# Chunk attention and a cosine router on one core: q moved from the GpSimd queue to the SP queue, the first loads reordered, the table fill moved

## The chip, the cores and the metric

The kernel runs on one core of one Trainium2 chip. The metric is the device time of one execution in microseconds. A core has five engines that run side by side, each with its own instruction stream: TensorE (PE) for matrix products, VectorE (DVE), ScalarE (ACT), GpSimd (POOL), and SyncE (SP), which here does nothing but issue transfers. All transfers run on 16 DMA engines that the queues share. A transfer issued by SP runs on the hardware queue, `q1` in the profile; one issued by GpSimd runs on the software queue, `q0`.

## What is computed

Two blocks follow each other. Attention within chunks of 64 rows, for 8 batches of 8 heads, 576 rows and 64 columns:

```python
batch, n_heads, seq, head_dim = (8, 8, 576, 64)
...
scores = scale * np.matmul(q_c, k_c.transpose(0, 1, 2, 4, 3))   # chunks of 64 rows
scores = scores - np.max(scores, axis=-1, keepdims=True)
attn = np.exp(scores)
attn = attn / (np.sum(attn, axis=-1, keepdims=True) + 1e-09)
out = np.matmul(attn, v_c)
```

The result, as 4608 tokens of 512 columns, goes to a router that sends each token to one of eight experts:

```python
logits = xn @ en.T / tau                   # normalized tokens and expert vectors
expert_idx = np.argmax(logits, axis=1)
...
for e in range(E):                         # E = 8, w1: 512 x 1024, w2: 1024 x 512
    mask = expert_idx == e
    h = np.maximum(x[mask] @ w1[e], 0.0)
    out[mask] = gate_w[mask, None] * (h @ w2[e])
```

Everything is float32.

## The kernel before

The attention stage walks over 36 tiles of 128 tokens, two chunks each. A batch of 576 rows is four and a half tiles. The tile of k and that of q hold all eight heads of 128 rows, with four buffers each, so that up to four tiles can be on their way. k is issued by SP, q by GpSimd. v is held for a whole batch, in two buffers that take turns, and loaded with one transfer for each head:

```python
tc.tile_pool(name="qk", bufs=4) as qk_p
...
def load_qk(t):
    for src, nm, eng in ((k, "kx", nc.sync), (q, "qx", nc.gpsimd)):
        x = qk_p.tile([P, H, Dh], FP32, tag=nm, name=nm)
        ...
            eng.dma_start(
                out=x[done : done + n],
                in_=src[b, :, s : s + n, :].rearrange("h p d -> p h d"),
            )
...
def load_v(b):
    t = v_sb[b % 2]
    for h in range(H):
        r0 = CH * (h % 2)
        nc.sync.dma_start(
            out=t[r0 : r0 + CH, h // 2, :, 0:Dh],
            in_=v[b, h].rearrange("(c k) d -> k c d", k=CH),
        )
    v_t[b] = t
```

In DRAM a row of q, k or v of one head is 64 floats, 256 bytes, so each of these transfers is made of pieces of 256 bytes. A tile of k or q is 1024 such pieces, 256 KB; v of one head of one batch is 576 pieces, 144 KB.

One pass of the main loop works on several tiles at different depths. It turns k and q of tile t+3 on TensorE (line 199), which frees their buffers, and loads tile t+7; it takes the scores of tile t+2 and the values of tile t, whose result x it writes to DRAM from GpSimd's queue. After the last tile, weights of the experts are loaded on the SP queue:

```python
for t in range(-3, NT + 3):
    if 0 <= t < NT:
        turn_a(t)
    if t + 3 < NT:
        turn_qk(t + 3)
        if t + 7 < NT:
            load_qk(t + 7)
        elif t + 7 == NT:
            load_first(w1_sb, w1_rows, KD, 0, nc.sync)
            load_first(w2_sb, w2_rows, KF, 0, nc.sync)
    ...
    if 0 <= t + 2 < NT:
        scores(t + 2)
    ...
    if 0 <= t < NT:
        values(t)                  # ends with the store of x, on GpSimd's queue
        b = (2 * t + 2) // NCB + 1
        if b not in v_t and b < B:
            load_v(b)              # the next batch, when this one begins
    ...
    put(1 if t < NT - 2 else 2)    # writes routed tokens into the table, from GpSimd
    if t == -2:
        turn_experts()
    if t == 0:
        clear_spots()
```

`clear_spots` fills the table `spots` in DRAM (2.3 MB) with a number that stands for "no row", by one transfer on the SP queue. The router's entries, of 64 bytes each, are then written over it by `put`; the first come six passes after t = 0. The start ahead of the loop:

```python
nc.sync.dma_start(out=emb, in_=moe_expert_emb)
nc.sync.dma_start(out=tau_sb, in_=moe_tau.unsqueeze(0).to_broadcast([E, 1]))
for t in range(2):
    load_qk(t)
norm_experts()
for x in v_sb:
    nc.vector.memset(x[:, :, :, Dh : Dh + 1], 1.0)
load_v(0)
for t in range(2, 4):
    load_qk(t)
load_v(1)
constants()
```

When all tokens are routed, the table is read by gathers on GpSimd's queue, which also loads the second set of weights, and the expert stage works through blocks of 128 tokens: `hidden` (line 635), `turn_h` (line 656) and `result` (line 668) on TensorE.

Of the kernel before, what the change touches and what calls it, by code (L numbers as in the profile page):

```python
# [19 lines left out]
CH = 64  # L20
# [5 lines left out]
def kernel(  # L26
# [11 lines left out]
    nc = tc.nc  # L38
    B, H, S, Dh = q.shape
# [7 lines left out]
    NCB = S // CH  # L47
# [32 lines left out]
    def load_first(buf, rows, n, i, eng):  # L80

        for s in range(2):
            e = (0, E - 1)[s]
            eng.dma_start(out=buf[s][i], in_=rows[:, e * n : e * n + n, :])
# [8 lines left out]
    with (  # L93
# [38 lines left out]
        def constants():  # L132
            nc.gpsimd.iota(tok_i, pattern=[[P, NT]], base=0, channel_multiplier=1)
            nc.gpsimd.iota(io_i, pattern=[[1, NST]], base=0, channel_multiplier=0)
            nc.gpsimd.iota(part_i, pattern=[[0, 1]], base=0, channel_multiplier=1)
            make_upper_triangular(nc, sltb, val=1.0, diag=False)
            nc.gpsimd.memset(onesb, 1.0)
            nc.gpsimd.memset(empty.bitcast(I32), NO_ROW)
            nc.gpsimd.memset(ones, 1.0)
            nc.gpsimd.memset(before, 0.0)  # L140
            nc.gpsimd.memset(jump[:, 1], 1.0)
            nc.gpsimd.memset(nb[:, 0:1], float((SPARE + N) // G))
            nc.gpsimd.tensor_copy(io, io_i)
            nc.gpsimd.tensor_copy(at, part_i)
            nc.gpsimd.tensor_scalar(pref, io[:, 0:E], -1.0, float(E), ALU.mult, ALU.add)
            nc.gpsimd.tensor_scalar(e_base, io[:, 0:E], float(N), None, ALU.mult)
            nc.gpsimd.tensor_scalar(second, at, float(G), None, ALU.is_ge)

            nc.gpsimd.tensor_scalar(at, at, 1.0 / G, None, ALU.mult)
            nc.gpsimd.tensor_tensor(at, at, second, ALU.subtract)  # L150
            nc.gpsimd.tensor_scalar(step, second, -2.0, 1.0, ALU.mult, ALU.add)
            nc.gpsimd.tensor_scalar(e_0, second, float(E - 1), None, ALU.mult)
            for x in xin_sb:
                nc.vector.memset(x, 0.0)
# [11 lines left out]
        qk_t, qkT, v_t, st = {}, {}, {}, {}  # L166

        def load_qk(t):

            for src, nm, eng in ((k, "kx", nc.sync), (q, "qx", nc.gpsimd)):  # L170
                x = qk_p.tile([P, H, Dh], FP32, tag=nm, name=nm)
                done = 0
                while done < P:
                    b, s = divmod(t * P + done, S)
                    n = min(P - done, S - s)
                    eng.dma_start(  # L176
                        out=x[done : done + n],
                        in_=src[b, :, s : s + n, :].rearrange("h p d -> p h d"),
                    )
                    done += n  # L180
                qk_t[nm, t] = x.rearrange("p h d -> p (h d)")

        def load_v(b):

            t = v_sb[b % 2]
            for h in range(H):
                r0 = CH * (h % 2)
                nc.sync.dma_start(  # L188
                    out=t[r0 : r0 + CH, h // 2, :, 0:Dh],
                    in_=v[b, h].rearrange("(c k) d -> k c d", k=CH),  # L190
                )
            v_t[b] = t

        def turn_qk(t):
            for nm in ("kx", "qx"):
                a = qk_t.pop((nm, t))
                ps = ps_t.tile([P, NPAIR, P], FP32, tag="tr", name="tr")
                for i in range(NPAIR):
                    nc.tensor.transpose(ps[:, i], a[:, i * P : i * P + P], ident)  # L199
                x = wk.tile([P, NPAIR, P], FP32, tag=nm + "T", name=nm + "T")  # L200
                if nm == "kx":
                    nc.scalar.copy(x, ps)
                else:
                    nc.vector.tensor_copy(x, ps)
                qkT[nm, t] = x
# [27 lines left out]
        def weights(t):  # L233
            a = st[t]["a"]
            nc.scalar.activation(a, a, AF.Exp, scale=scale)

        def turn_a(t):
            d = st[t]
            ps = ps_t.tile([P, NPAIR, P], FP32, tag="tr", name="tr")
            for i in range(NPAIR):  # L240
                nc.tensor.transpose(ps[:, i], d["a"][:, i].rearrange("p r k -> p (r k)"), ident)  # L241
            aT = wk.tile([P, NPAIR, P], FP32, tag="aT", name="aT")
            nc.scalar.copy(aT, ps)
            d["aT"] = aT
# [31 lines left out]
        def turn_x(t):  # L276
            d = st[t]
            ps = ps_t.tile([P, KD, P], FP32, tag="tr", name="tr")
            for c in range(KD):
                nc.tensor.transpose(ps[:, c], d["x"][:, c * P : c * P + P], ident)  # L280
            xT = wk.tile([P, KD, P], FP32, tag="xT", name="xT")
            nc.scalar.copy(xT, ps)  # L282
            d["xT"] = xT

        def logits(t):
            d = st.pop(t)
            for c in range(KD):
                nc.tensor.matmul(  # L288
                    rt_ps[:, 0, batch_of[t][1]],
                    lhsT=d["xT"][:, c],  # L290
                    rhs=enT[:, c],
                    start=(c == 0),
                    stop=(c == KD - 1),
                )
# [74 lines left out]
        def put(n):  # L369

            for at, m in to_put[:n]:
                ins = nc.gpsimd.indirect_dma_start(  # L372
                    out=spots,
                    out_offset=bass.IndirectOffsetOnAxis(ap=at, axis=0),
                    in_=m,
                    in_offset=None,
                    bounds_check=SPARE - 1,
                    oob_is_err=False,
                )
                tc.declare_no_dep(ins.ins, group="spots", reason="each token has its own place")  # L380
                tc.add_to_no_dep_group("spots", ins.ins)
            del to_put[:n]
# [73 lines left out]
        def norm_experts():  # L456

            junk = one.tile([P, D], FP32, tag="junk", name="junk")
            nc.scalar.activation(junk[0:E], emb, AF.Square, accum_out=emb_sq)
            nc.scalar.activation(emb_n, emb_sq, AF.Sqrt)  # L460
            nc.vector.tensor_scalar(emb_n, emb_n, 1e-6, None, ALU.add)
            nc.vector.reciprocal(emb_n, emb_n)
            nc.vector.reciprocal(tau_sb, tau_sb)
            nc.vector.tensor_scalar(emb, emb, emb_n, tau_sb, ALU.mult, ALU.mult)

        def turn_experts():
# [2 lines left out]
                nc.tensor.transpose(ps[:, c, 0:E], emb[:, c * P : c * P + P], ident[0:E, 0:E])  # L469
            nc.vector.tensor_copy(enT, ps[:, :, 0:E])  # L470

        nc.sync.dma_start(out=emb, in_=moe_expert_emb)
        nc.sync.dma_start(out=tau_sb, in_=moe_tau.unsqueeze(0).to_broadcast([E, 1]))
        for t in range(2):
            load_qk(t)
        norm_experts()
        for x in v_sb:
            nc.vector.memset(x[:, :, :, Dh : Dh + 1], 1.0)
        load_v(0)
        for t in range(2, 4):  # L480
            load_qk(t)
        load_v(1)
        constants()
        ends = {sum(sizes[: b + 1]) - 1: b for b in range(len(sizes))}
        for t in range(-3, NT + 3):
# [10 lines that stand above are left out]
            if t == NT:  # L496
                turn_x(t - 1)
            if 0 <= t - 2 < NT:
                logits(t - 2)
            if 0 <= t + 2 < NT:  # L500
                scores(t + 2)
            if t - 3 in ends:
                place(ends[t - 3])
            if 0 <= t - 1 < NT - 1:
                turn_x(t - 1)
            if 0 <= t < NT:
                values(t)
                b = (2 * t + 2) // NCB + 1
                if b not in v_t and b < B:
                    load_v(b)  # L510
            if 0 <= t + 2 < NT:
                weights(t + 2)
            if t - 2 in ends:
                pick(ends[t - 2])

            put(1 if t < NT - 2 else 2)
            if t == -2:
                turn_experts()
            if t == 0:
                clear_spots()  # L520
        groups()
        places(0, XBUF + 1)
# [241 lines left out]
```

## Time and profile before

| | |
|---|---|
| median of three runs | 806.37 us |
| lowest and highest | 802.37 and 807.18 us |
| span of the profiled run | 810.2 us |
| TensorE busy | 743.9 us, 92% of the span |
| hardware queue q1 | 101,136 packets, 84.18 MB |
| software queue q0 | 16,528 packets, 47.17 MB |
| HBM read and written | 383.07 MB and 21.80 MB |

The page gives the busy time of each engine and then cuts the span into 40 equal slices; a digit is the busy share of a slice in tenths. `PEclk` is the clock that TensorE was granted, `DMA` the mean busy share of the 16 DMA engines, `GB/s` what they moved. Packets of two queues on one DMA engine can be open at the same time, so shares of two queues can add up to over 100%. The timeline lists an engine's instructions in order, with the idle time before each and what ended it.

### The profile page before, as it was taken

The numbers are of one execution on the slowest core, as the hardware profiler recorded it, in microseconds if no ns is written. First come the engines' busy times: TensorE is split into PE (matmuls) and PEld (weight loads), VectorE is DVE, ScalarE is ACT, GpSimd is POOL, SyncE is SP. The second block draws the span as 40 slices with busy tenths as digits, with TensorE's granted clock in tenths as the row PEclk, the third lists the DMA queues.
The fourth block names the chain that finished last, engine by engine and source line by source line (L and its number), as shares of the span: only waits on it lengthen the run. The fifth ranks groups of instructions, "written<-read, shape, count | busy, mean of one in ns | idle before, by whom it ended". The sixth has DMA issues, their size and how long they took to land.

```text
span 810.2 us, 15342 instructions
## 1 busy us (share of the span) xinstructions
PE 743.9 (92%) x6033; PEld 367.7 (45%) x6033; DVE 251.7 (31%) x703; ACT 290.7 (36%) x520; POOL 221.3 (27%) x270
## 2 busy tenths in 40 slices
PE   2799999985569999999999999999999999999994
PEld 2688888874124333343343333343333343333331
DVE  2467777775221121121121121121121122122100
ACT  3345455441142243243243243333334334334102
POOL 4235556545420211211211311311211221221220
PEclk9999999995778999999999999999999999999998
DMA  9999999993670100115583416688530444312140
GB/s 177 234 264 246 238 251 234 258 399 133 233 247 1 51 27 27 53 59 202 189 305 131 155 61 229 253 328 323 169 118 27 144 144 131 140 44 79 72 150 9
DMA packets 117739, 132.37 MB, mean 163 GB/s; under 512 B 79860, under 2 KB 83252, under 8 KB 117664
## 3 DMA queue, kind: packets, MB, share of 16 engines
q1 hardware_dynamic: 101136, 84.18, 35.9%
q0 software_dynamic: 16528, 47.17, 18.4%
q8 instruction: 49, 0.80, 0.4%
q14 instruction: 26, 0.21, 0.1%
HBM read 383.07 MB, written 21.80 MB: 500 GB/s over the span
## 4 chain that ended last, share of the span: by engine, by line
PE 83%; DMA 4%; issue 3%; DVE 3%; SPq 3%; POOL 1%; ACT 0%; POOLq 0%; DVEq 0%; ACTq 0%
PE y_ps L668 31%; PE h_ps L635 29%; PE ht_ps L656 4%; PE rt_ps L288 4%; PE pv L255 3%; PE tr L280 3%; PE tr L199 3%; PE sc L215 2%; SPq L188 2%; PE tr L241 2%; PE x_ps L604 2%; DMA w<-in_moe_w_dram 2%; DMA spot<-spots,src_row 1%; DVE x L266 1%; SPq L176 1%
## 5 line engine op out<-in xcount | busy, mean ns | idle before, releaser
L635 PE MATMUL h_ps<-w,xbT 128*64 128x512 f32 x1184 | 267.9, 604 | 9.9 <-DMA w<-in_moe_w_dram 6.6
L668 PE MATMUL y_ps<-w,hT 128*64 128x512 f32 x1184 | 262.0, 595 | 0.0
L635 PEld LDWEIGHTS h_ps<-w,xbT 128*64 128x64 f32 x1184 | 88.5, 140 | 181.3 <-issue 174.4
L677 POOL DMA_INDIRECT out_dram<-y,spot x37 | 37.8, 1022 | 441.6 <-ACT y L676 425.7
L668 PEld LDWEIGHTS y_ps<-w,hT 128*64 128x64 f32 x1184 | 81.8, 137 | 154.6 <-issue 154.1
L644 ACT ACTIVATE h<-h_ps 128x512 f32<-128x512 f32 x37 | 22.1, 597 | 259.2 <-PE h_ps L635 231.8
L646 DVE TENSOR_SCALAR h<-h_ps 128x512 f32<-128x512 f32 x37 | 25.6, 691 | 225.4 <-PE h_ps L635 225.4
L676 ACT ACTIVATE y<-y_ps,gate 128x512 f32<-128x512 f32 x37 | 25.4, 687 | 126.1 <-PE y_ps L668 126.1
L660 DVE COPY hT<-ht_ps 128x512 f32<-128x512 f32 x37 | 25.6, 692 | 126.9 <-PE ht_ps L656 123.5
L623 ACT ACT_TABLE_LOAD x37 | 47.5, 1283 | 0.7
L618 ACT ACT_TABLE_LOAD x37 | 47.5, 1283 | 0.7
L527 POOL DMA_INDIRECT xin<-x_rows,spot x40 | 41.4, 1034 | 22.2 <-issue 11.3
L656 PEld LDWEIGHTS ht_ps<-ident,h 128*128 128x128 f32 x296 | 31.7, 141 | 30.4 <-issue 29.2
L282 ACT COPY xT<-tr 128x512 f32<-128x512 f32 x36 | 21.1, 586 | 64.8 <-PE tr L280 46.1
L527 POOL DMA_INDIRECT spot<-spots,src_row x40 | 40.4, 1009 | 13.9 <-issue 11.6
L288 PE MATMUL rt_ps<-enT,xT 128*128 128x8 f32 x288 | 37.6, 257 | 5.8 <-DVE m L310 5.7
L199 PE MATMUL tr<-ident,kx 128*128 128x128 f32 x144 | 24.2, 296 | 18.4 <-DMA kx<-in_k_dram 18.4
L288 PEld LDWEIGHTS rt_ps<-enT,xT 128*128 128x128 f32 x288 | 37.5, 203 | 7.7 <-DVE m L310 4.1
L656 PE MATMUL ht_ps<-ident,h 128*128 128x128 f32 x296 | 40.6, 280 | 0.1
L176 POOL DMA_DIRECT2D qx<-in_q_dram x40 | 35.3, 886 | 19.0 <-PE tr L199 17.8
L372 POOL DMA_INDIRECT spots<-m,dest x36 | 36.7, 1019 | 11.4 <-issue 10.6
L273 POOL DMA_DIRECT2D x_rows<-x x36 | 20.3, 565 | 70.0 <-DVE x L266 55.8
(123 smaller groups left out, 659.3 us busy)
## 6 DMA issues: line engine op xcount, KB each, us to landing
w<-in_moe_w_dram SPq DMA_DIRECT2D x160, 2048.0 KB
v<-in_v_dram SPq DMA_DIRECT2D x64, 144.0 KB
x_rows<-x POOLq DMA_DIRECT2D x36, 256.0 KB
qx<-in_q_dram POOLq DMA_DIRECT2D x32, 256.0 KB
kx<-in_k_dram SPq DMA_DIRECT2D x32, 256.0 KB
w<-in_moe_w_dram POOLq DMA_DIRECT2D x4, 2048.0 KB
spots<-empty SPq DMA_DIRECT2D x1, 2312.0 KB
qx<-in_q_dram POOLq DMA_DIRECT2D x8, 128.0 KB
```

Of the source, the lines that this page charges most:

```text
L176: eng.dma_start(out=x[done : done + n], in_=src[b, :, s : s + n, :].rearrange("h p d -> p h d"),)
L199: nc.tensor.transpose(ps[:, i], a[:, i * P : i * P + P], ident)
L288: nc.tensor.matmul(rt_ps[:, 0, batch_of[t][1]], lhsT=d["xT"][:, c], rhs=enT[:, c], start=(c == 0), stop=(c == KD - 1),)
L372: ins = nc.gpsimd.indirect_dma_start(out=spots, out_offset=bass.IndirectOffsetOnAxis(ap=at, axis=0), in_=m, in_offset=None, bounds_check=S ...
L527: nc.gpsimd.indirect_dma_start(out=dst, out_offset=None, in_=table, in_offset=bass.IndirectOffsetOnAxis(ap=at, axis=0), bounds_check=rows - 1,
L618: nc.scalar.activation(rn, rn, AF.Sqrt)
L623: nc.scalar.activation(sh, sh, AF.Exp, accum_out=gate)
L635: nc.tensor.matmul(ps[G * s : G * s + G], lhsT=d["xT"][:, c, G * s : G * s + G], rhs=w1_sb[s][j % 2][:, c, fh * 512 : fh * 512 + 512], sta ...
L646: nc.vector.tensor_scalar(dst, ps, 0.0, None, ALU.max)
L656: nc.tensor.transpose(ps[:, c], d["h"][:, f0 : f0 + P], ident)
L668: nc.tensor.matmul(ps[G * s : G * s + G], lhsT=d["hT"][:, c, G * s : G * s + G], rhs=w2_sb[s][j % 2][:, c], start=(c == 0), stop=(c == KF ...
L677: ins = nc.gpsimd.indirect_dma_start(out=out, out_offset=bass.IndirectOffsetOnAxis(ap=spot[:, j, E : E + 1].bitcast(I32), axis=0), in_=y, ...
```

## The change

It has three parts. q goes back to the SP queue, where k and v already are, so that GpSimd no longer issues loads of q. The first loads stand in the order in which the tiles use them: k and q of tile 0 come ahead of the expert vectors, and of v of batch 0 the two chunks that tile 0 needs are loaded ahead of the other seven; v of batch 1 moves from the start into the loop (pass t = -1). And the fill of the table is issued three passes later (t = 3 instead of t = 0). The aim is that the first tiles are there sooner and that the start has less to move.

```diff
         def load_qk(t):
-
-            for src, nm, eng in ((k, "kx", nc.sync), (q, "qx", nc.gpsimd)):
+            for src, nm in ((k, "kx"), (q, "qx")):
...
-                    eng.dma_start(
+                    nc.sync.dma_start(
...
-        def load_v(b):
+        def load_v(b, c0=0, c1=NCB):
...
-                    out=t[r0 : r0 + CH, h // 2, :, 0:Dh],
-                    in_=v[b, h].rearrange("(c k) d -> k c d", k=CH),
+                    out=t[r0 : r0 + CH, h // 2, c0:c1, 0:Dh],
+                    in_=v[b, h, CH * c0 : CH * c1].rearrange("(c k) d -> k c d", k=CH),
...
+        load_qk(0)
         nc.sync.dma_start(out=emb, in_=moe_expert_emb)
         nc.sync.dma_start(out=tau_sb, in_=moe_tau.unsqueeze(0).to_broadcast([E, 1]))
-        for t in range(2):
-            load_qk(t)
+        load_qk(1)
         norm_experts()
         for x in v_sb:
             nc.vector.memset(x[:, :, :, Dh : Dh + 1], 1.0)
-        load_v(0)
-        for t in range(2, 4):
-            load_qk(t)
-        load_v(1)
+
+        load_v(0, 0, 2)
+        load_qk(2)
+        load_v(0, 2, NCB)
+        load_qk(3)
         constants()
...
-            if t == 0:
+            if t == -1:
+                load_v(1)
+            if t == 3:
                 clear_spots()
```

The instructions of TensorE, VectorE and ScalarE stay the same, in the same order.

## The prediction

> **What bounds the kernel now.** I read the page's slices first, to see which stage the change touches; then TensorE's timeline of the start; then the DMA queues in three windows, because every part of the change moves a transfer and none moves an instruction of a compute engine.
>
> The slices, each 20.25 us long, and the packet counts of the page:
>
> ```profile
> PE   2799999985569999999999999999999999999994
> ...
> PEclk9999999995778999999999999999999999999998
> DMA  9999999993670100115583416688530444312140
> GB/s 177 234 264 246 238 251 234 258 399 133 233 247 1 51 27 27 53 59 202 189 305 131 155 61 229 253 328 323 169 118 27 144 144 131 140 44 79 72 150 9
> DMA packets 117739, 132.37 MB, mean 163 GB/s; under 512 B 79860, under 2 KB 83252, under 8 KB 117664
> ```
>
> The attention stage is the first nine and a half slices. TensorE is full in it from the third slice on, and the DMA engines are full from the first. Both are candidates for the bound. From slice 13 on the expert stage runs on full TensorE with little DMA; nothing of the change reaches it except by when it starts.
>
> TensorE's timeline of the start (start, length, what; in brackets the idle time before it):
>
> ```profile
> 10.20 1.06 PE L199 MATMUL tr<-ident,qx 128*128 128x128 f32 x4
> ...
> 22.61 1.09 PE L199 MATMUL tr<-ident,kx 128*128 128x128 f32 x4 [9.77 <-DMA kx<-in_k_dram]
> ...
> 32.51 1.08 PE L199 MATMUL tr<-ident,kx 128*128 128x128 f32 x4 [2.30 <-DMA kx<-in_k_dram]
> ...
> 37.18 0.60 PE L199 MATMUL tr<-ident,kx 128*128 128x128 f32 x4
> ...
> 45.36 0.60 PE L199 MATMUL tr<-ident,kx 128*128 128x128 f32 x4
> ```
>
> Tiles 0 and 1 are turned by 11 us, tile 2 waits until 22.61 because its k stands on the SP queue behind all eight loads of v of batch 0, and tile 4 waits until 32.51. Tile 5 follows at 37.18, tile 7 at 45.36; from there no wait for a load stands in the timeline. At the other end tile 35, the last, is turned at 170.99, and the first gather of the expert stage starts on GpSimd at 201.91.
>
> The DMA queues, first from 19 to 26 us (only the hardware queue, loads of k and v in 256-byte rows), then from 60 to 160 us (steady tiles), then from 230 to 238 us (only the software queue, in 4 KB packets):
>
> ```profile
> DMA packets 5269, 1.32 MB, mean 188 GB/s; under 512 B 5269, under 2 KB 5269, under 8 KB 5269
> ...
> q1 hardware_dynamic: 5269, 1.32, 99.6%
> ```
>
> ```profile
> DMA packets 53019, 24.48 MB, mean 245 GB/s; under 512 B 49773, under 2 KB 50114, under 8 KB 52997
> ...
> q1 hardware_dynamic: 48666, 12.18, 68.8%
> q0 software_dynamic: 4331, 11.99, 43.5%
> ```
>
> ```profile
> DMA packets 764, 3.06 MB, mean 383 GB/s; under 512 B 16, under 2 KB 16, under 8 KB 764
> ...
> q0 software_dynamic: 764, 3.06, 100.0%
> ```
>
> The reader is to see two prices. k and v each have 36,864 rows of 256 B (9.44 MB), together 73,728 packets, and the page counts only 79,860 packets under 512 B in the whole run: q, with as many rows, is not among them. So GpSimd's queue carries q in large packets: q0 moved 11.99 MB in 4,331 packets between 60 and 160 us. The hardware queue has one packet for each 256 B row. Alone, it moves 188 GB/s; large packets of the software queue alone move 383 GB/s. With these two rates the steady window adds up: 12.18 MB / 188 GB/s = 64.8 us and 11.99 / 383 = 31.3 us, 96 of its 100 us. The DMA engines were nearly as full as TensorE (97.25 us busy of 100 in that window). The pace is one tile in 4.44 us (18 stores of x from 60 to 140 us).
>
> **What the Trainium skill says.** "DMA: Bandwidth & Descriptors", section "Why small descriptors are slow (HBM only)": each packet has a fixed overhead, and putting neighbouring descriptors into one packet takes part of it away, which is worth it at 256 B or less. The trace agrees in direction and shows more than that page's 27%: 188 against 383 GB/s. The same page, "Queues, rings and completion order": a DMA engine changes between queues only at packet boundaries. The trace agrees: in the packet records a 256 B packet takes 18 ns (median) from 23 to 26 us with the software queue silent or nearly so, and 28 ns from 10 to 15 us between 4 KB packets. The same page, "Issuing engines are not separate DMA queues": moving a load to another issuer saves only issue time. Here that is incomplete, since the issuer also decides the packet size. "TensorE: Matmul & The Clock Gate", section "What's actually happening": an idle stretch halves the TensorE clock in windows of about 3.4 us. The trace agrees: four transposes take 1.06 to 1.09 us up to 32.51 and 0.60 us from 37.18 on.
>
> **The change part by part.**
>
> 1. First loads in order of use, v of batch 0 split (2 of 9 chunks first). Compute starts earlier. Bytes until tile 4 is there: five tiles of k and q at 0.524 MB, plus 1.18 MB of v of batch 0, 3.80 MB; at 188 GB/s 20.2 us, and with 2.5 us until the first data, 22.7 us instead of 32.51. But the next tiles need v of batch 1 also: until tile 7, 8 x 0.524 + 2 x 1.18 = 6.55 MB at 188 GB/s = 34.9 us, plus three stores of x (0.262 MB / 383 GB/s = 0.7 us each) and 2.5 us: 39.4 us instead of 45.36. The lead is thus 9.8 us at tile 4 and 6 us at tile 7. The wait of 9.77 us goes away as such, but part of it was time in which the DMA engines fetched later tiles ahead, so it is not a gain of 9.77 us.
>
> 2. q to the SP queue. This removes 40 issues of q from GpSimd (mean 886 ns, 35.3 us), which lay beside other work: no wait for GpSimd is at the end of the chain there. It adds 36,864 packets of 256 B in place of some 2,300 of 4 KB. Over all of q: 9.44 / 188 = 50.2 us instead of 9.44 / 383 = 24.6 us of all 16 engines, 25.6 us more. In the steady tile: k, q and v are 0.786 MB at 188 GB/s = 4.18 us, x is 0.7 us, together 4.88 us against 4.44 us now. TensorE would wait for loads, about 0.4 us in each tile.
>
> 3. The fill begun three tiles later. 2.37 MB at some 335 GB/s (the mean of 37 to 43 us, when it ran) is 7.1 us of DMA time. It is the same work, moved out of the start. The rows that it clears are first written three tiles after it is issued, some 14 us, so it should be done by then.
>
> The sum, as the time at which the last tile of k and q has landed: 28.3 MB / 188 GB/s = 150.6 us, 31 stores of x at 0.7 us = 21.7 us, the fill 7.1 us, and 2.5 us: 181.9 us. The same sum for the kernel before is 18.87 / 188 + 9.44 / 383 + 21.7 + 7.1 + 2.5 = 156.3 us, and the packet records show 163.4 us, so it may be some us short. Tile 35 is turned at 170.99 now, with its k there 7.6 us earlier; it would be turned at about 182, 11 us later. What follows it takes 30.9 us to the first gather and should take the same. The weights loaded after it on the SP queue (8.4 MB, at 400 GB/s with the stores of x about 25 us) end at about 208, just ahead of that gather at 213. So 806.4 + 11 = 817; I take one us off for a rate a little over 188 and predict 816.
>
> **The rivals.**
>
> (a) TensorE stays the bound. If rows of k and q go at 215 GB/s when nothing disturbs them, tile 35 lands at 182 - 19 = 163 us, TensorE keeps its 4.44 us, and the 6 to 10 us won at the start stay: about 798. For it: stretches of a microsecond reach 218 GB/s in the packet records, and in 60 to 160 us the queue's loads often waited for a buffer to come free. Against it: over seven full microseconds the mean was 188, and even in the steady stretch each load's last packet came 2 to 5 us after its issue, so the queue was never empty for long.
>
> (b) The waits for loads halve TensorE's clock. v of a batch (1.18 MB, 6 us) goes ahead of the next k and q on one queue; if that makes a gap of over 2 us in each batch, windows at half the clock cost 1 to 2 us in each of eight batches, and the weights come late into the gathers: 825 to 832. For it: the start of the kernel before does just this. Against it: four buffers let k and q run ahead across a load of v.
>
> (c) The SP queue's issuing becomes the bound. Before, k took a median 1.15 us an issue and v 0.715; with q a tile has 2 x 1.15 + 1.8 x 0.715 = 3.6 us of issue, under 4.44. Part of it is the queue being full, as the first two k took 0.5 us each. I give this little.
>
> **Range and chances.** The middle follows from 188 GB/s; 215 gives 798, with the lead at the start kept, and rival (b) up to 830. Range 799 to 830. Two per cent are 16.1 us: slower than 822.5 needs an end of loading 5 to 6 us later still (some 181 GB/s) or rival (b); I give it 0.30. Faster than 790.2 would need more than the whole gain at the start, 0.06. Within 2%: 0.64.
>
> **What would show it.** Right: q's packets all in q1, some 36,900 more under 512 B; tile 4 turned at 22 to 24 us; then waits of TensorE for kx or qx in the middle of the stage, together over 10 us, with GB/s in slices 3 to 8 near 215; tile 35 turned at 178 to 188. Wrong: tile 35 turned before 171, or a steady pace of 4.44 us without waits for loads, which would mean that 256 B rows go faster than they did from 19 to 26 us; or a late end with no waits for loads, which would mean that the cost comes from the fill or from the tail.

## The result, and the profile after

The changed kernel takes 815.48 us (median of four runs, 813.11 to 816.67), beside 804.61 us of the kernel before, measured along with it: 1.013 of it, 95% interval 1.0086 to 1.0175, or 10.9 us more. The prediction was 816 us. The number fell where it was forecast; the way to it did not, and that is the use of this case.

One thing about the comparison first. The profile shown ahead of the prediction is of an execution of 812.1 us, longer than the timed runs of that kernel (802.4 to 807.2). A second profile of the same kernel, of 803.4 us, is used from here on (run `e1_before_again` below). The two differ only ahead of the expert stage: tile 35 is turned at 165.91 instead of 170.99 us, and the first gather starts at 192.98 instead of 201.91. The profile of the changed kernel is of the slowest of its four runs (816.7 us).

The page of the changed kernel, the lines that answer to those of before:

```profile
PE   5896999986559999999999999999999999999993
...
PEclk9996999995688999999999999999999999999997
DMA  7999999997670100115583416798530443413140
GB/s 158 231 276 221 223 232 241 229 314 296 230 247 1 51 26 27 53 41 218 176 317 130 152 53 232 255 329 319 172 113 27 146 141 130 142 40 101 57 141 9
DMA packets 152427, 132.37 MB, mean 162 GB/s; under 512 B 116852, under 2 KB 120244, under 8 KB 152352
```

Small packets rose from 79,860 to 116,852, by 36,992; q's 36,864 rows are now in them. TensorE is busy sooner (slices 1 and 2), but slice 4 has dropped to 6, and there the granted clock is down too. GB/s in slices 3 to 8 lies between 221 and 276.

TensorE's timeline of the changed kernel (start, length, what; the idle time before it), with the turns of tiles 4, 7, 11, 12, 13, 14, 25 and 35:

```profile
25.55 0.60 PE L198 MATMUL tr<-ident,kx 128*128 128x128 f32 x4
...
39.17 0.63 PE L198 MATMUL tr<-ident,kx 128*128 128x128 f32 x4 [1.82 <-DMA kx<-in_k_dram]
...
58.44 0.60 PE L198 MATMUL tr<-ident,kx 128*128 128x128 f32 x4
...
62.13 0.66 PE L240 MATMUL tr<-ident,a 128*128 128x128 f32 x4
68.53 1.09 PE L198 MATMUL tr<-ident,kx 128*128 128x128 f32 x4 [5.75 <-DMA kx<-in_k_dram]
70.67 1.09 PE L198 MATMUL tr<-ident,qx 128*128 128x128 f32 x4 [1.05 <-DMA qx<-in_q_dram]
...
77.29 1.06 PE L198 MATMUL tr<-ident,kx 128*128 128x128 f32 x4
...
82.48 0.60 PE L198 MATMUL tr<-ident,kx 128*128 128x128 f32 x4
...
128.57 0.63 PE L198 MATMUL tr<-ident,kx 128*128 128x128 f32 x4
131.18 0.63 PE L198 MATMUL tr<-ident,qx 128*128 128x128 f32 x4 [1.98 <-DMA qx<-in_q_dram]
...
174.88 0.60 PE L198 MATMUL tr<-ident,kx 128*128 128x128 f32 x4
```

The same of the kernel before in its second profile, tiles 11, 12, 14 and 35:

```profile
62.90 0.60 PE L199 MATMUL tr<-ident,kx 128*128 128x128 f32 x4
...
66.99 0.60 PE L199 MATMUL tr<-ident,kx 128*128 128x128 f32 x4
...
75.62 0.60 PE L199 MATMUL tr<-ident,kx 128*128 128x128 f32 x4
...
165.91 0.60 PE L199 MATMUL tr<-ident,kx 128*128 128x128 f32 x4
```

In the changed kernel there is a wait of 5.75 us for k of tile 12, one of 1.05 us for its q, and then transposes of 1.06 to 1.09 us instead of 0.60: half the clock, up to tile 13. The SP queue just before (start, length of the issue) shows what stood ahead of that tile:

```profile
43.90 1.56 SPq L157 DMA_DIRECT2D spots<-empty  x1
45.55 3.48 SPq L175 DMA_DIRECT2D kx<-in_k_dram  x1
49.12 3.05 SPq L175 DMA_DIRECT2D qx<-in_q_dram  x1
52.29 10.88 SPq L187 DMA_DIRECT2D v<-in_v_dram  x8
63.26 1.51 SPq L175 DMA_DIRECT2D kx<-in_k_dram  x1
```

The fill, then tile 11, then all of v of batch 2, and only then k of tile 12. Engine times by stretch (stretch, length, busy time of PE and its loads, of DVE, ACT and POOL, then granted clock, DMA share, GB/s), first of the changed kernel, then of the kernel before in its second profile:

```profile
60.00:68.00 8.00, 2.79 (x76) 2.22 (x75) 2.65 (x6) 1.69 (x3) 2.85 (x4) 0.85 0.99 210
68.00:82.00 14.00, 12.42 (x178) 11.15 (x178) 5.98 (x15) 3.35 (x6) 1.80 (x3) 0.60 1.14 220
82.00:160.00 78.00, 75.40 (x1610) 68.47 (x1607) 62.10 (x153) 39.29 (x73) 29.13 (x40) 1.00 0.99 234
```

```profile
60.00:68.00 8.00, 8.00 (x176) 7.36 (x176) 6.28 (x13) 4.05 (x9) 5.13 (x6) 1.00 1.20 233
68.00:82.00 14.00, 13.93 (x310) 12.70 (x308) 11.30 (x29) 7.06 (x14) 8.46 (x12) 1.00 1.18 258
82.00:160.00 78.00, 76.03 (x1616) 68.59 (x1609) 62.29 (x154) 39.19 (x72) 46.68 (x61) 1.00 1.15 251
```

Between 60 and 82 us the changed kernel has 254 matmuls, the kernel before 486. From 82 to 160 us the two do nearly the same work. So in this profile it is mostly one accident and not a slower pace. From the turns of the tiles: at tile 11 the changed kernel leads by 4.5 us (58.44 against 62.90), at tile 14 it is 6.9 us behind (82.48 against 75.62), at tile 35 9.0 us (174.88 against 165.91). From there to the first gather it takes 30.5 us against 27.1, from the gather to the third block of the expert stage the same in both, and from the last matmul to the end 13.06 against 11.54. 6.9 + 2.1 + 3.4 + 1.5 is 13.9; the rest of the expert stage gives 0.6 back, and 13.3 us is the distance of the two profiles (814.7 and 801.4). The 3.4 us cannot be put down to the change: in the first profile of the kernel before the same stretch took 30.9 us. The 1.5 us can; it comes back in every run below that has no loads of q on GpSimd's queue.

### The profile page after: what moved, and what is told of

It reads as the page before. It is cut to its first block, busy times and chain, and to the rows that moved or that the text cites. A ratio compares the mean times of both kernels' runs of the same rounds, so it can differ in the third digit from the quotient of the medians.

```text
span 814.7 us, 15357 instructions
## 1 busy us (share of the span) xinstructions
PE 747.1 (92%) x6033; PEld 368.9 (45%) x6033; DVE 251.6 (31%) x703; ACT 289.4 (36%) x520; POOL 185.9 (23%) x230
## 2 busy tenths in 40 slices
DMA packets 152427, 132.37 MB, mean 162 GB/s; under 512 B 116852, under 2 KB 120244, under 8 KB 152352
## 4 chain that ended last, share of the span: by engine, by line
PE 83%; DMA 7%; issue 3%; DVE 3%; SPq 2%; POOL 1%; ACT 0%; POOLq 0%; DVEq 0%; ACTq 0%
PE y_ps L670 31%; PE h_ps L637 29%; PE ht_ps L658 4%; PE rt_ps L287 4%; PE tr L198 3%; DMA qx<-in_q_dram 3%; PE sc L214 3%; PE pv L254 2%; PE tr L279 2%; PE tr L240 2%; PE x_ps L606 2%; DMA w<-in_moe_w_dram 2%; DMA spot<-spots,src_row 1%; SPq L187 1%; DMA kx<-in_k_dram 1%
## 5 line engine op out<-in xcount | busy, mean ns | idle before, releaser
L606 PE MATMUL x_ps<-ident,xin 128*128 128x128 f32 x148 | 22.8, 278 | 13.4 <-DMA xin<-x_rows,spot 13.4
```

What stands on the lines that cost most here:

```text
L606: nc.tensor.transpose(ps[:, c], t[:, c * P : c * P + P], ident)
```

## The experiments

Each group ran on one chip, beside the kernel before: 804.36 us in the first group (e1 to e4), 811.84 in the second (e5 to e8), 811.45 in the third (e9 to e12). So only ratios are compared. The changed kernel's 1.013 was measured beside a kernel before of 804.6 us; it was not run on the chips of the second and third group. Times of tiles can be compared within a group. Where a run of the second or third group is set beside e1, the chip may make part of the difference; the first profile of the kernel before, with 812.1 us, lies nearer to the level of these groups, and its tile 35 came at 170.99.

| run | what | median, us | ratio to before, 95% interval | tile 12, tile 35 turned at, us |
|---|---|---|---|---|
| e1_before_again | kernel before | 803.37 | one run | 66.99, 165.91 |
| e2_fill_at_0 | changed, fill at pass 0 | 814.65 | 1.0125 (1.0085 to 1.0166) | 69.88, 175.04 |
| e3_q_gpsimd | changed, q on GpSimd's queue | 805.12 | 1.0006 (0.9980 to 1.0031) | 66.17, 166.06 |
| e4_q_sp_only | before, q on SP | 810.99 | 1.0097 (1.0063 to 1.0132) | 63.74, 166.26 |
| e5_order_only | before, new order and split | 814.38 | 1.0023 (1.0005 to 1.0040) | 71.74, 173.03 |
| e6_kq_gpsimd | changed, k and q on GpSimd's queue | 814.14 | 1.0015 (0.9996 to 1.0035) | 70.25, 179.50 |
| e7_k_gpsimd_too | before, k on GpSimd's queue too | 813.58 | 1.0011 (0.9990 to 1.0031) | 66.84, 174.33 |
| e8_q_act | changed, q on ScalarE's queue | 817.81 | 1.0081 (1.0054 to 1.0108) | 69.08, 173.62 |
| e9_v_whole | changed, split of v undone | 812.98 | 1.0014 (0.9994 to 1.0034) | 63.31, 170.90 |
| e10_no_q | changed, q not loaded | 801.58 | 0.9871 (0.9838 to 0.9904) | -, 159.99 |
| e11_spread_v | changed, v spread over four passes | 842.66 | 1.0374 (1.0321 to 1.0426) | 67.13, 196.92 |
| e12_spread_v_q_gpsimd | the same with q on GpSimd's queue | 837.50 | 1.0283 (1.0234 to 1.0333) | 66.08, 197.52 |

The theories, named as in the expectations: A, one late tile, because the fill and v of batch 2 now stand together ahead of it. B, the sum: q in 256-byte packets gives the DMA engines more to do ahead of tile 12, wherever the lumps stand. C, the late fill eats the lead. D, the order within one queue, not the packets. A gives way to B if moving the lumps does not help.

**e1_before_again**, no edit.

> The kernel before, unchanged, for a second profile. Its first profiled run took 812.1 us, more than the median of 804.6 us of its other runs, so it may show some waits that are not typical. Expected: a span of some 803 us; tile 12 turned at 66 to 70 us and tile 35 at 164 to 171 us, so that the distance to the changed kernel (tile 35 at 174.9) is 5 to 10 us and not 3.9.

Tile 12 at 66.99, tile 35 at 165.91 us, span 801.4 us: as expected, and the distance to the changed kernel is 9.0 us.

**e2_fill_at_0**

```diff
-            if t == 3:
+            if t == 0:
                 clear_spots()
```

> The changed kernel with the fill of the table back at pass 0. Theory A (one late tile: fill and v of batch 2 now stand one behind the other on the queue ahead of k and q of tile 12, so that TensorE waits 5.75 us there and then works two tiles at half its clock): the burst is split, no wait over 2 us at tile 12, about 804 to 808 us. Theory B (256-byte packets of q: the queue simply has more work ahead of tile 12 wherever the fill stands): tile 12 is as late as before, 813 to 817 us.

As slow as the changed kernel. Tile 12 was as late (69.88 against 68.53 us), but the wait came at tile 8, and a second one, again with half the clock, at tile 34:

```profile
49.81 1.09 PE L198 MATMUL tr<-ident,kx 128*128 128x128 f32 x4 [6.15 <-DMA kx<-in_k_dram]
...
167.24 1.09 PE L198 MATMUL tr<-ident,kx 128*128 128x128 f32 x4 [2.70 <-DMA kx<-in_k_dram]
```

At tile 14 (78.51 us) it was 4.0 us ahead of the changed kernel and 2.9 behind e1; the other 6 us were lost at tiles 34 and 35.

Theory A falls as the cause of the loss: it is not that the fill stands next to v. Its move brings or costs nothing that can be measured here.

**e3_q_gpsimd**

```diff
-            for src, nm in ((k, "kx"), (q, "qx")):
+            for src, nm, eng in ((k, "kx", nc.sync), (q, "qx", nc.gpsimd)):
```

> The changed kernel with q on GpSimd's queue again; new order of the first loads and late fill are kept. Theory A: k of tile 12 still stands behind fill and v of batch 2, but with half the other tiles' bytes on the queue, so the wait at tile 12 shrinks to 0 to 3 us: 803 to 810 us. Theory B: without the 256-byte packets of q the whole lead of the start is kept, 796 to 801 us.

No slower than before, and no faster. With q on GpSimd's queue the other two parts together bring nothing: the lead of 8 us at tile 2 is 3.2 at tile 7 (40.19 against 43.40) and 0.8 at tile 12. The loss of the change needs q on SP. Theory B had forecast more, that the whole lead stays, and this missed. Tile 12 was late here too, with half the clock after it, as theory A said:

```profile
66.17 1.01 PE L198 MATMUL tr<-ident,kx 128*128 128x128 f32 x4 [1.87 <-DMA kx<-in_k_dram]
```

A lead of 2.8 us at tile 11 was 1.9 us behind at tile 14. So the fill and v in one lump cost something with q on either queue; with q on GpSimd's queue it cost no more than the lead.

**e4_q_sp_only**

```diff
-            for src, nm, eng in ((k, "kx", nc.sync), (q, "qx", nc.gpsimd)):
+            for src, nm, eng in ((k, "kx", nc.sync), (q, "qx", nc.sync)):
```

> The kernel before with q on the SP queue and nothing else of the change. Theory A: no fill next to v of batch 2, so no single late tile: within 3 us of the kernel before, 803 to 808 us. Theory B: q's packets cost DMA time all along, 812 to 822 us, with waits for kx and qx in several places.

0.97% slower, by q's move alone, 1 us short of theory B's lower figure. So the late fill and the split are not needed for a loss. Its profile is of its fastest run (808.6 us) and shows the same kind of accident at tile 16, with half the clock after it:

```profile
81.82 0.63 PE L199 MATMUL tr<-ident,kx 128*128 128x128 f32 x4 [1.10 <-DMA kx<-in_k_dram]
83.96 0.63 PE L199 MATMUL tr<-ident,qx 128*128 128x128 f32 x4 [1.51 <-DMA qx<-in_q_dram]
```

But this accident only ate a lead. With q on SP tile 2 was turned at 16.02 instead of 22.25 us without any new order, tile 14 was 3.2 us ahead of e1, tile 18 2.2 us behind and tile 35 0.3 us behind. Of the 5.3 us between the two profiles 2.7 lie between tile 35 and the first gather, a stretch that differs by 3.9 us between two profiles of the kernel before, and 1.6 at the very end. So e4 shows that q's move costs time, but not that late loads make all of it.

**e5_order_only**

```diff
 # the changed kernel, with q on GpSimd's queue as in e3
-            if t == 3:
+            if t == 0:
                 clear_spots()
```

> The kernel before with only the new order of the first loads and the split of v (q on GpSimd's queue, fill at pass 0). Theory B (the DMA engines have no room up to tile 12, so a lead won at the start by reordering is lost again until then): tile 2 turned some 8 us sooner than before, tile 13 within 2 us of it, 800 to 806 us, no measurable change. Theory C (the late fill eats the lead in the kernel with q on GpSimd's queue and late fill, which took 805.1 us): the lead of 3 to 6 us at tile 8 stays, 796 to 800 us.

1.0023. Tile 2 was turned at 14.33 us; tile 8 then waited 6.04 us for k, behind the fill. The lead of the start is lost with the early fill as with the late one, which speaks for theory B (tile 13 at 75.83 is 2.1 us after the first profile of the kernel before); theory C falls.

**e6_kq_gpsimd**

```diff
-            for src, nm, eng in ((k, "kx", nc.sync), (q, "qx", nc.gpsimd)):
+            for src, nm, eng in ((k, "kx", nc.gpsimd), (q, "qx", nc.gpsimd)):
```

> The changed kernel with both k and q on GpSimd's queue, in 4 KB packets; v and the fill stay on SP. Theory B (the size of the packets sets the DMA time): k costs 25 us less of DMA time over the stage, the lead of the start is kept past tile 12, no waits for kx or qx after it: 794 to 800 us. Theory D (what hurts q on SP is the order of one queue, in which v and the fill stand ahead of q, and not the packets): little better than with q alone on GpSimd's queue, 801 to 807 us. GpSimd then issues 0.9 us for k, 0.9 for q, 0.6 for x and 1.0 for a table entry in each tile, 3.4 of 4.3 us; if it falls behind, the pace gets worse.

**e7_k_gpsimd_too** is the same line in the kernel before.

> The kernel before with k on GpSimd's queue as well; order and fill as before. Theory B: less DMA time and k no longer behind v on one queue; tile 2 turned at 10 to 14 us instead of 22, 794 to 800 us. Theory D: tile 2 is early as well, but values of tile 0 wait for v, which now shares the engines with more 4 KB packets: 798 to 804 us. The two differ in the middle: DMA share under 1.0 from 60 to 160 us under theory B.

Both missed. Theory B as I had widened it (the more large packets, the faster) is wrong: nothing was gained, although both runs end 5.6 us sooner after the last matmul than the kernel before (6.0 against 11.5 us). What lies ahead of that took 7 to 8 us longer. The waits for k and q are nearly gone (1.2 us in all in e7 from 10 to 176 us), but TensorE's waits list of e7 in that stretch (who waited for what: us in total, times, longest) begins with another cause:

```profile
PE pv L255 <- issue: 5.1, 4, 1.7
PE tr L199 <- issue: 3.4, 1, 3.4
PE sc L215 <- issue: 2.5, 2, 1.8
```

Some of these stretches on its timeline:

```profile
34.87 0.59 PE L199 MATMUL tr<-ident,kx 128*128 128x128 f32 x2 [3.38 <-issue]
...
51.79 0.34 PE L255 MATMUL pv<-v,aT 64*64 64x65 f32 x6 [1.39 <-issue]
```

"issue" is idle time for which the profile shows nothing that TensorE waits for. Over this stretch it adds up to 0 us in the changed kernel, in e2 and in e8, to at most 0.5 in e4, e5 and e9, to 1.7 in e1, 2.6 in e3, 8.3 in e6 and 11.8 in e7. It tends to grow with the loads on GpSimd's queue, but not strictly (2.2 in e10, which has none there). e6 waited 6.3 us for v besides.

The packet records of the traces say what TensorE lacked. A stretch can begin in the middle of a group: the first of the two lines above stands between the four transposes of one tile of k, which all need the same loads. Instructions themselves are loaded by transfers: the queue q8 carries 49 packets of 16 KB, of kind "instruction", in this stage one every 6 to 7 us. Each of the 17 stretches of e6 and e7 between 10 and 178 us ends 1.3 to 1.7 us after one of these packets has landed (the two above 1.5 us after packets that landed at 33.37 and 50.26 us), and so do 10 of the 11 in the other profiles. So TensorE had very probably run out of instructions. Why they come late more often beside more loads on GpSimd's queue is not shown.

**e8_q_act**

```diff
-            for src, nm in ((k, "kx"), (q, "qx")):
+            for src, nm, eng in ((k, "kx", nc.sync), (q, "qx", nc.scalar)):
```

> The changed kernel with q on ScalarE's hardware queue: 256-byte packets as on SP, but a queue of its own. Theory B (packets): as slow as the changed kernel, 811 to 818 us, with tile 12 late again. Theory D (one queue in order): q no longer stands behind fill and v, k has half the bytes ahead of it; as fast as with q on GpSimd's queue, 802 to 807 us. ScalarE's issue of q may hold up its copies by 0.5 us in each tile, which would add to either.

0.81% slower, with tile 12 late again:

```profile
69.08 1.09 PE L198 MATMUL tr<-ident,kx 128*128 128x128 f32 x4 [3.79 <-DMA kx<-in_k_dram]
```

Theory D falls in its full form: q has a queue of its own, and yet the run is not as fast as with q on GpSimd's queue (1.0023 in e5 on the same chip, 1.0006 in e3 on another). Standing behind v and the fill can be a part of the cost at most: the wait is shorter than the 5.75 us of the changed kernel, but 1.0081 and 1.0130 come from different chips and their intervals overlap. Of the 3.4 us between e8 and e5, 1.5 are again at the very end. That it includes some holding up of ScalarE's copies stays possible.

**e9_v_whole**

```diff
-        load_v(0, 0, 2)
+        load_v(0)
         load_qk(2)
-        load_v(0, 2, NCB)
```

> The changed kernel with v of batch 0 loaded whole ahead of tile 2 (the split undone: 8 issues fewer). In its trace the eight small loads took 5.6 us to issue on SP, as long as eight large ones, and the DMA engines idled. If the lead of the start is lost anyway at tile 12: tile 3 turned some 2 to 5 us sooner, tile 12 as late as with the split, the time the same within 3 us (ratio to before 1.008 to 1.015). If the start decides the time: 3 to 5 us less (1.004 to 1.008).

A surprise: 1.0014. Both of my cases underrated it. The DMA queues from 6 to 12 us show why, first in the changed kernel, then in e9:

```profile
DMA packets 2415, 0.58 MB, mean 97 GB/s; under 512 B 2415, under 2 KB 2415, under 8 KB 2415
```

```profile
DMA packets 4929, 1.23 MB, mean 205 GB/s; under 512 B 4929, under 2 KB 4929, under 8 KB 4929
```

SP takes a median 0.63 us to issue one head's v in the changed kernel's start, whether it is 128 rows or 448, and 0.64 us for all 576 in e9. The eight small loads are 5.61 us of issue for 0.26 MB, and the DMA engines stand half idle. From 2 to 20 us the changed kernel moves 3.10 MB and e9 3.82 MB. In e3, with the split and with q on GpSimd's queue, the same stretch of 6 to 12 us moves 213 GB/s: there q fills the hole. In e9 tile 12 is turned at 63.31 us after a wait of 2.69 us, 5.2 us sooner than in the changed kernel. The mechanism is shown in the traces. Its size is not settled: 1.013 and 1.0014 come from different chips, and e4, which has no split either, lost 0.97% on the first group's chip.

**e10_no_q**

```diff
-            for src, nm in ((k, "kx"), (q, "qx")):
+            for src, nm in ((k, "kx"),):
...
-                a = qk_t.pop((nm, t))
+                a = qk_t.pop(("kx", t)) if nm == "qx" else qk_t["kx", t]
```

> The changed kernel without the loads of q: k is turned twice in each tile and stands in q's place. It leaves out 9.44 MB of loads; scores, routing and result are not those of the reference, so the expert stage may take a block more or less, and the stage is read by when tile 35 is turned. If DMA time is what q costs: no wait for kx after the start, one tile in 4.3 us from tile 3 on, tile 35 turned at 155 to 162 us, against 174.9 in the changed kernel and 165.9 in the second profile of the kernel before. If something else holds the stage (GpSimd, the copies), tile 35 stays at 166 or later.

Without q's 9.44 MB tile 35 is turned at 159.99 us, 14.9 us sooner than in the changed kernel, 5.9 sooner than in e1 (on another chip) and 11.0 sooner than in the first profile of the kernel before, with 2.6 us of waits for loads from 10 to 176 us. So q's loads are what holds tile 35 back, and the compute engines alone would allow a shorter stage than that of the kernel before. The run takes away q's bytes, packets and issues together; it does not tell them apart.

**e11_spread_v**

```diff
+        to_load = []
...
-                    load_v(b)
+                    to_load.extend((b, h) for h in range(H))
...
-                load_v(1)
+                to_load.extend((1, h) for h in range(H))
+            for b, h in to_load[:2]:
+                load_v(b, heads=(h,))
+            del to_load[:2]
```

> The changed kernel with the loads of v of a batch spread over four passes, two heads in each, so that k and q of tile 12 have the fill but only a quarter of v of batch 2 ahead of them. Same bytes, same packets. If the loss is the burst (fill and v in one lump at a small lead): tile 12 comes some 4 us sooner, the wait is 0 to 2 us, no stretch at half the clock, ratio to before 1.000 to 1.006. If the loss is the sum of the bytes: the waits move to tiles 13 to 16, ratio 1.009 to 1.015.

**e12_spread_v_q_gpsimd**, the same edit on e3.

> The attempt at a better version: new order, late fill and v spread over four passes as in the run above, with q on GpSimd's queue in large packets. The same without the spread took 1.0006 of the kernel before and still lost its lead at tiles 9, 12 and 13. If the lumps cost it the lead: 0.990 to 0.996. If TensorE's own pauses without a shown cause near 50 us and the pace of the DMA engines decide: 0.998 to 1.003.

Their times say nothing of the question, by a flaw of the edit: the last two heads of v of batch 7 came after the expert weights (8.4 MB) on the SP queue, and TensorE waited for them 20.4 and 19.6 us at the end of the stage. Up to tile 30 the traces can be read. In e11 tile 12 was turned at 67.13 us, 1.4 us sooner than in the changed kernel, but now v came late (waits of 3.86 us at 45.40 and 3.00 us at 74.09), and tile 29 was turned at 147.97, against 147.26 (on another chip). Spread or in a lump, the bytes were late, as theory B has it. But e12, with q on GpSimd's queue, turned tile 29 no sooner (149.31), so this pair does not show that q's packets are to blame. No version that was tried and computes the whole result beats the kernel before.

## Why the prediction was right, and where it was not

**The direction and the part at fault: right.** q on SP costs time: 1.0130 in the changed kernel and 1.0006 with q back on GpSimd's queue (e3), and 0.97% for q's move alone (e4). Leaving q out brings tile 35 forward by 14.9 us (e10), and another hardware queue does not restore the time (e8). Of the losses of the changed kernel, of e4 and of e8 some 1.5 us each are not DMA time but the longer end.

**Step 2's size, wrong.** It said that TensorE would wait "about 0.4 us in each tile". From tile 14 to 35 the changed kernel takes 92.4 us for 21 tiles, 4.40 us each, against 4.30 in e1 and 4.39 in the first profile of the kernel before, and TensorE waits for loads at two of these tiles only (1.98 and 0.97 us). This is close to what the prediction had named as a sign of being wrong. I also took 4.44 us as the pace now, from a profile slower than most. The mis-sized term is 188 GB/s for 256-byte rows. The queues of the changed kernel from 60 to 160 us:

```profile
DMA packets 70245, 22.97 MB, mean 230 GB/s; under 512 B 68562, under 2 KB 68886, under 8 KB 70226
...
q1 hardware_dynamic: 67910, 17.03, 82.5%
q0 software_dynamic: 2316, 5.66, 17.2%
```

If 5.66 MB at 383 GB/s take 14.8 us, 17.03 MB went in 85.2 us: 200 GB/s. e9 moved 212 GB/s from 2 to 20 us, nearly all in such rows; with 212, as an estimate, the prediction's sum for a tile is 0.786 MB / 212 GB/s + 0.7 us = 4.41 us. I had read the rate from one window of seven microseconds and, in rival (a), held 215 to be a rare peak.

**What took its place** is rival (b), to which I gave too little: a wait at one tile, and half the clock after it. At tile 12 TensorE waited 6.8 us, and the half clock took some 4.5 us more: a lead of 4.5 us at tile 11 was 6.9 us behind at tile 14 (tile 12 to 13 took 8.76 us). One later wait, 1.98 us for q at 131 us, makes most of the rest up to tile 35: 9.0 us behind e1, where the sum said 11.

**Step 1, half right.** Tile 7 was turned at 39.17 (predicted 39.4). But tile 4 was turned at 25.55, not at 22 to 24, because the split's issues on SP left the DMA engines half idle. If ratios of different chips may be compared, e9 says that this made most of the loss: with q on SP nothing else fills the hole. Against it stands e4, which lost 0.97% without the split; the share of the split stays open. That was rival (c), to which I gave "little"; I had counted it only against the steady pace.

**Step 3** said that the fill is the same work wherever it stands: e2 and e5 agree. It did not see that the fill and v would meet at tile 12; e2 shows that without this meeting the wait comes at tile 8.

**The tail** "should take the same" 30.9 us to the first gather. It took 30.5. Against e1's 27.1 that is 3.4 more, but two profiles of the kernel before differ by more than this; TensorE is at half the clock up to the end of this stretch in all three (from 185.1 us on in the changed kernel, from 180.7 in e1 and 182.3 in the first profile). What the prediction did not have is the 1.5 us at the very end.

**Luck in the number.** The prediction added 11 us, counted from tile 35 of a profile of 812.1 us, to a median of 806.4 from faster runs. From that profile tile 35 came only 3.9 us later (174.88 after 170.99), from e1 9.0 later, and the longer end was not in the sum. The misses cancel: 816 is closer than its terms. Of the signs that the prediction set itself, the packets and the waits of over 10 us came out (10.5 for k and 4.3 for q from 20 to 200 us). GB/s fell less than said (221 to 276 in slices 3 to 8, not near 215), and tile 35 at 174.9 lay outside 178 to 188.

**A reading of packets.** 18 ns for a 256-byte packet alone and 28 ns beside 4 KB packets show that it takes longer in company. They do not show that an engine changes queues only between packets: that shares of the queues add up to over 100% says that packets of both can be open at once.

## What to carry to other kernels

Where the DMA engines are nearly full, an early start through reordering can be a loan: the bytes up to some later tile are the same, and of a lead of 8 us at tile 2 only 0.8 was left at tile 12 (e3). Look for stretches of low GB/s before splitting a load, since an issue of v took SP the same 0.63 us for a small load as for a large one. And a wait of 6.8 us on TensorE cost some 11 us here, because half the clock came after it. Last, two executions of the same kernel differed by 3.9 us between tile 35 and the first gather: a difference of that size between two single profiles shows nothing of a change.

## What the runs showed of the hardware that was not expected

- The last instruction that holds the end up is GpSimd's closing DRAIN, and its length goes with which loads GpSimd had issued: 7.43 us with q on its queue (e1), 8.65 us with neither (changed kernel), 2.95 us with k and q (e7). From the last matmul to the end it is 11.5 us in all five profiles with q alone on GpSimd's queue, 13.1 us in all seven with neither, and 6.0 us in both with k and q. So 1.5 us of the change's loss lies at the very end. Why was not found.
- Issuing v of one head takes SP about 0.63 us for 128, 448 or 576 rows.
- Moving more loads into GpSimd's large packets took away TensorE's waits for them, but idle time without a wait for data grew to 11.8 us (e7), and nothing was gained.
- Such idle time ended 1.3 to 1.7 us after a 16 KB packet of instructions had landed, in 27 of 28 stretches of all profiles. The 28th (0.17 us, in e9) ended 2.6 us after one.
